# Six tiles of a causal convolution, each cut into five overlapping blocks of its own, in a kernel that TensorE bounds

## The chip, the core and the metric

The kernel runs on one core of a Trainium2 chip. A core has five engines with a queue of instructions each: TensorE (PE; its weight loads are listed apart as PEld), VectorE (DVE), ScalarE (ACT), GpSimd (POOL) and SyncE (SP). Each queue runs in order; the engines meet through semaphores only. All large transfers of this kernel but the first weights are issued from SP's queue. The metric is the device time of one execution in microseconds (us).

## The reference

```python
def _attn_ref(x, weight):                 # x (8, 4096, 192), weight (8, 7)
    w = softmax of weight over its 7 taps  # one set of taps per head, 24 channels a head
    x_pad = 6 rows of zeros in front of each sequence
    out[b, s, h, g] = sum over k of w[h, k] * x_pad[b, s + k, h, g]

def _moe_ref(x, w_in, w_out):             # x (32768, 192), w_in (192, 2048), w_out (2048, 192)
    h = x @ w_in
    g = h * np.cos(h)
    return g @ w_out
```

The second function works on the 32768 rows that the first gives.

## The kernel before

**Tiles and units.** The 32768 rows are 64 tiles of 512 rows, and two tiles are a unit of 1024. For each tile `t` the first product (`mm1`, L503) makes eight pieces `h0` to `h7`: each is 2 x 128 columns of `w_in` against 512 rows, six matmuls over 64 rows of the array, in pairs. Each piece fills one of three double banks (`h_pool`, three buffers). ScalarE takes its cosine (`gcu`, L510, "s0" to "s7"), VectorE multiplies (L514), and the double bank is free again. The second product (`mm2_step`, L552) has 64 steps per tile, each two matmuls on the two row halves; step k of a tile needs piece k // 4 within each half of the steps and one half of `w_out`: steps 0 to 15 the first, 16 on the second. Its two banks are emptied by VectorE ("Q") and ScalarE ("P") (L571) before the next tile's first step.

**The convolution before the change.** The convolution gives each tile as a bf16 transpose `cT`, channels on partitions, which `mm1` reads. There are three ways to it:

- Unit 0 (tiles 0 and 1) in the head of the kernel (`conv_first`, `turn_first`, `conv_rest`): banded 128 x 128 matrices on TensorE, and for tile 0 transposes on TensorE too.
- Units 1 to 3 (tiles 2 to 7): `load_unit` brings the 1024 rows, `load_edges` the 8 rows before each block of 128; `cast_unit` casts both on POOL; `conv_part` (L229) multiplies four heads with the bands over 128 rows into a double bank, twice per unit ("d" and "c"), and ScalarE copies it out (L239); `double_unit` (L307) writes each 64-channel square twice; `turn_unit` (L326) transposes 27 blocks by a transfer; `mend_edges` (L394) puts the first six columns of each block right.
- Units 4 to 31: five blocks of 112 rows, each loaded with the 16 rows before it, by TensorE (`conv_unit`, L277: 16 matmuls over 64 rows and 120 columns; L294 copies them out; two transposes L317 by transfer, "X" and "x", one for each row half), and 464 rows by ScalarE and POOL ("taps" L356, `conv_raw`, `spread_raw`).

**The order is written by hand.** `PE_FIRST`, `ACT_FIRST` for the first tiles and `PE_ORDER`, `ACT_ORDER` for the rest are lists of words; nothing is scheduled afterwards. `h3` is a piece of the first product, `m7` seven steps of the second, `c1`/`c2` the two halves of a convolution, `L`, `K`, `X`, `x`, `T`, `R`, `U` a unit's load, cast, transposes, raw transpose, raw convolution and its spreading, `O` a store; in `ACT` lists `s` is cosine and product, `e..` a copy of a convolution out of its bank, `a..` a tap. A convolution takes one of the three double banks in turn with the pieces.

**Turns.** [...] Between the first and the second half of a convolution (`conv_unit`) and of a tile's 64 steps, an instruction in SP's queue (`Turn`, L196) waits for the first half's last matmul, and the second half waits for it. It stands in SP's queue in order with the loads, transposes and stores.

Of the kernel before, what the change touches and what calls it, by code (L numbers as in the profile page):

```python
# [16 lines left out]
def kernel(  # L17
# [35 lines left out]
    HALF = WN // 2  # L53

# [30 lines left out]

    def load_edges(u, queue=nc.sync):
        queue.dma_start(out=x_tiles[u][:, UB, :],
                          in_=xf[u * U - 8 : u * U - 8 + U, :].rearrange("(n t) d -> n t d", t=128)[:, 0:16, :])
# [25 lines left out]
    load_unit(0, 0, NB)  # L114
# [11 lines left out]


# [9 lines left out]

# [14 lines left out]

# [35 lines left out]

# [14 lines left out]


    bf, xk = {}, {}

    def cast_unit(u, n0=0, n1=UB + 1, copy=nc.gpsimd.tensor_copy):
        if u >= FIRST_RAW:
            xk[u] = xk_pool.tile([128, NC * (UB + 1), 64], BF16, name="xk")
            for n0, n1 in ((NPB, UB + 1), (0, NPB)):  # L210
                copy(out=xk[u][:, NC * n0 : NC * n1].rearrange("p (k n) m -> p k n m", k=NC),  # L211
                     in_=x_tiles[u][:, n0:n1].rearrange("p n (m k) -> p k n m", k=NC))
            if u % UPS == 0:
                nc.gpsimd.memset(xk[u][0 : 128 - OP, 0 : NC * NPB : NPB], 0.0)
            return
        if n0 == 0:
            bf[u] = xb0 if u == 0 else xbf_pool.tile([128, UB + 1, D], BF16, name="x_bf")
        o = 1 if u == 0 else 0
        copy(out=bf[u][:, n0 + o : n1 + o, :].rearrange("p n (h k r) -> p (n h) k r", k=NC, r=R),  # L219
             in_=x_tiles[u][:, n0:n1, :].rearrange("p n (h r k) -> p (n h) k r", k=NC, r=R))  # L220

    ct_tiles = {}
    have = {("whole", 0, 0)}

    def conv_mm(u, c, ps, i, rows, n0, n1, prev=0, **flags):

        h = 4 * c + i
        rhs = bf[u][rows, n0:n1, h * G : (h + 1) * G].rearrange("p n (k r) -> p n k r", k=NC)
        return nc.tensor.matmul(  # L229
            out=ps[i // 2][:, 0 : (n1 - n0) * 2 * G].rearrange("p (n k i r) -> p i n k r", n=n1 - n0, k=NC, i=2)[:, i % 2],  # L230
            lhsT=band[rows, h, 128 if prev else 0 : 256 if prev else 128],
            rhs=rhs, skip_group_check=True, **flags)

    def conv_out(u, c, ps, n0, m0, m1, copy, banks=(0, 1)):

        for b in banks:
            w0 = (2 * c + b) * 2 * R
            o = ct_tiles[u][:, m0:m1, :, 0, w0 : w0 + 2 * R].rearrange("p n k w -> p (n k) w")
            copy(o, ps[b][:, (m0 - n0) * 2 * G : (m1 - n0) * 2 * G].rearrange("p (m w) -> p m w", w=2 * R))  # L239
# [7 lines left out]

    def conv_part(u, c, banks, whole=False):


        ps = banks()
        nb = UB + 1
        for i in range(4):
            conv_mm(u, c, ps, i, slice(0, 128), 0, nb, start=i % 2 == 0, stop=i % 2 == 1)
        if u == 1 and c == 0:
            spread_taps(ps[1][:, nb * 2 * G : nb * 2 * G + K])
        yield
        yield
        if u not in ct_tiles:
            ct_tiles[u] = ct_pool.tile([128, UB + 1, NC, 2, 64], BF16, name="ct")  # L260
        for b in range(2):
            conv_out(u, c, ps, 0, 0, nb, nc.scalar.copy, banks=(b,))
            if b and u == 1 and c == 0:
                nc.scalar.copy(tap, ps[1][:, nb * 2 * G : nb * 2 * G + K])
            if b:
                have.add(("conv", u, c))
            yield

    def conv_unit(u, banks):
# [32 lines left out]
    def double_unit(u):  # L302

        assert {("conv", u, 0), ("conv", u, 1)} <= have
        have.add(("double", u))
        ct = ct_tiles[u]
        nc.gpsimd.tensor_copy(out=ct[:, :, :, 1, :], in_=ct[:, :, :, 0, :])  # L307

    def turn_unit(u, n0=0, n1=UB + 1, part=0):
        if u >= FIRST_RAW:  # L310
            assert {("conv", u, 0), ("conv", u, 1)} <= have
            if part == 0:
                cT[u] = cT_pool.tile([128, NC * (UB + 1) * 128], BF16, name="cT")
            else:
                have.update((("whole", u, 0), ("whole", u, 1)))
            to = cT[u][:, 0 : NC * CW].rearrange("p (n s t) -> p s n t", s=2, t=OP)
            nc.sync.dma_start_transpose(out=to[:, part],  # L317
                                        in_=ct_bufs[u % 2][0:OP, part : part + 2 * NC * NPB].rearrange("p s m -> p (s m)"))
# [405 lines left out]
```

## Time and profile before

| what | us |
|---|---|
| median, lowest and highest of the runs | 705.1, 704.99, 705.26 |
| the profiled execution, and its span | 705.18, 703.5 |
| TensorE busy | 697.0 (99%) |
| ScalarE busy | 644.4 (92%) |
| VectorE busy | 642.4 (91%) |
| POOL busy | 503.7 (72%) |
| granted TensorE clock | 0.999 |

The span runs from the first to the last instruction. A busy TensorE isn't TensorE at its peak, as matmuls overlap; so the chain of work that ended last and the starts of consecutive groups tell more than the busy time. In a timeline's row stand the start, the length, the engine, the line, the operation, what is written and read, the shape, the number of instructions, and in brackets an idle time before it with what ended it. "SPq" rows are transfers that SP issues: the length is that of the issue, not of the transfer.

### The profile page before, as it was taken

To read this page: it belongs to the slowest core of one execution; us is meant where nothing else is said; L and a number is where in the kernel's file an instruction comes from. 1 tells how busy PE (TensorE), PEld (TensorE's weight loads), DVE (VectorE), ACT (ScalarE), POOL (GpSimd) and SP (SyncE) were. 2 spreads that over 40 slices of the span, in tenths; PEclk is the share of its full clock that TensorE was granted. 3 is DMA by queue.
4 is the path that set the end of the run, shared out by engine and by line. 5 is a ranking of instruction groups with operands and counts; after the bars stand their busy time and mean duration, and the time that the engine had idled before them with its cause. 6 is when DMAs were issued, how large, how long until landed. Compare 5 with 4: busy or idle time off the path is not lost.

```text
span 703.5 us, 26826 instructions
## 1 busy us (share of the span) xinstructions
PE 697.0 (99%) x11830; PEld 512.8 (73%) x11830; DVE 642.4 (91%) x598; ACT 644.4 (92%) x831; POOL 503.7 (72%) x214
## 2 busy tenths in 40 slices
PE   8999999999999999999999999999999999999997
PEld 4677777777777777777777777777777777777776
DVE  6889999999999999999999999999999999999996
ACT  7889999999999999999999999999999999999875
POOL 6524478977778877778877688877789778799400
PEclk9999999999999999999999999999999999999999
DMA  8964456667667768676656577577665576874331
GB/s 214 234 167 97 120 135 143 138 147 164 138 153 146 131 145 176 134 152 131 147 152 153 150 159 129 140 161 150 143 147 132 145 174 137 153 127 95 92 91 47
DMA packets 228292, 100.09 MB, mean 142 GB/s; under 512 B 156240, under 2 KB 227792, under 8 KB 228176
## 3 DMA queue, kind: packets, MB, share of 16 engines
q1 hardware_dynamic: 227464, 97.40, 62.7%
q8 instruction: 92, 1.51, 0.9%
q0 software_dynamic: 416, 0.79, 0.7%
q14 instruction: 24, 0.20, 0.1%
q10 hardware_dynamic: 296, 0.20, 0.1%
HBM read 31.36 MB, written 25.17 MB: 80 GB/s over the span
## 4 chain that ended last, share of the span: by engine, by line
PE 96%; DMA 1%; DVE 1%; POOL 0%; SPq 0%; ACT 0%; issue 0%; POOLq 0%
PE o_ps L552 48%; PE h L503 46%; PE h L277 2%; DMA wo_f<-in_moe_w_out_dram 1%; PE h L552 0%; SPq L124 0%; PE h L229 0%; DVE band L415 0%; POOL wo L120 0%; POOL mask L159 0%; DVE ct L438 0%; PE o_ps L432 0%; ACT mask L164 0%; DVE diag L404 0%; DVE prod L401 0%
## 5 line engine op out<-in xcount | busy, mean ns | idle before, releaser
L514 DVE TENSOR_TENSOR g<-h,cs 128x1024 bf16<-128x1024 f32 (+1 forms) x513 | 604.9, 1216 | 27.9 <-ACT cs L510 24.5
L510 ACT ACTIVATE cs<-h 128x1024 bf16<-128x1024 f32 (+1 forms) x513 | 511.0, 1021 | 44.0 <-PE h L503 30.6
L552 PEld LDWEIGHTS <-g 64*128 64x128 bf16 x8192 | 354.2, 94 | 102.2 <-issue 1.0
L552 PE MATMUL o_ps<-wo,g 64*128 64x192 bf16 x8128 | 420.6, 243 | 0.1
L503 PE MATMUL h<-cT,w 64*128 64x512 bf16 (+1 forms) x3078 | 407.0, 376 | 0.8 <-DVE g L514 0.4
L503 PEld LDWEIGHTS <-w 64*128 64x128 bf16 x3078 | 147.6, 94 | 75.0 <-issue 1.8
L211 POOL CAST xk<-x_f 128x768 bf16<-128x768 f32 (+1 forms) x56 | 76.4, 1367 | 113.9 <-DMA x_f<-in_x_dram 109.3
L363 POOL TENSOR_TENSOR raw_prod<-rT,tap 128x2784 f32<-128x2784 bf16 x28 | 135.3, 4832 | 0.2
L370 POOL TENSOR_TENSOR raw_prod<-raw_prod,pa 128x2088 f32<-128x2088 f32 x28 | 129.1, 4609 | 2.2
L356 ACT ACTIVATE pa<-rT,tap 128x348 f32<-128x348 bf16 x168 | 94.6, 580 | 0.0
L374 POOL TENSOR_TENSOR raw_prod<-raw_prod 128x1392 f32<-128x1392 f32 x28 | 87.9, 3138 | 2.2
L571 DVE COPY o_sb<-o_ps 128x384 f32<-128x384 f32 x62 | 34.6, 557 | 23.7 <-PE o_ps L552 23.5
L377 POOL TENSOR_TENSOR ro<-raw_prod 128x696 bf16<-128x696 f32 x28 | 46.5, 1660 | 2.2
L294 ACT CAST ct_buf<-h 112x480 bf16<-112x480 f32 x56 | 28.6, 562 | 4.1 <-PE h L277 0.6
L571 ACT COPY o_sb<-o_ps 128x384 f32<-128x384 f32 x64 | 30.8, 482 | 0.1
L277 PE MATMUL h<-xk,band 64*112 64x120 bf16 x448 | 21.2, 213 | 0.0
L277 PEld LDWEIGHTS <-band 64*112 64x112 bf16 x448 | 18.0, 127 | 0.0
L219 POOL CAST x_bf<-x_f 128x768 bf16<-128x768 f32 (+2 forms) x5 | 9.1, 1812 | 7.0 <-DMA x_f<-in_x_dram 6.9
L307 POOL COPY ct<-ct 128x1728 bf16<-128x1728 bf16 x3 | 4.9, 1630 | 8.9 <-ACT ct L239 8.9
L394 POOL COPY cT<-cT 128x144 bf16<-128x144 bf16 x3 | 0.9, 308 | 13.5 <-DMA cT<-ct 13.5
L136 PE MATMUL o_ps<-zero 128*128 128x512 bf16 x21 | 7.2, 492 | 1.3 <-DVE zero L131 1.3
L239 ACT CAST ct<-h 128x432 bf16<-128x432 f32 x12 | 5.9, 530 | 0.4 <-issue 0.4
(66 smaller groups left out, 52.7 us busy)
## 6 DMA issues: line engine op xcount, KB each, us to landing
out_dram<-o_sb SPq DMA_DIRECT2D x63, 384.0 KB, 3.7
x_f<-in_x_dram SPq DMA_DIRECT2D x28, 480.0 KB, 5.5
x_f<-in_x_dram SPq DMA_DIRECT2D x56, 192.0 KB, 2.7
cT<-ro SPq DMA_DIRECT2D x112, 87.0 KB, 2.3
x_f<-in_x_dram SPq DMA_DIRECT2D x4, 384.0 KB, 5.6
wo_f<-in_moe_w_out_dram SPq DMA_DIRECT2D x4, 384.0 KB, 7.9
x_f<-in_x_dram SPq DMA_DIRECT2D x2, 768.0 KB, 5.2
cT<-ct_buf SPq DMA_TRANSPOSE x56, 4.0
```

The costliest lines, as they stand in the source:

```text
L211: copy(out=xk[u][:, NC * n0 : NC * n1].rearrange("p (k n) m -> p k n m", k=NC), in_=x_tiles[u][:, n0:n1].rearrange("p n (m k) -> p k n m", ...
L277: return nc.tensor.matmul(out=ps[h // 4][0:OP, 0 : NPB * 4 * G].rearrange("p (m i r) -> p i m r", m=NC * NPB, i=4)[:, h % 4], lhsT=band[si ...
L356: mul(pa[u][:, j, part], tap_window(u, j)[:, part], tap[:, j : j + 1])
L363: nc.gpsimd.tensor_tensor(out=p, in0=tap_window(u, PA, K), in1=tap[:, PA:K].rearrange("p (j a b) -> p j a b", a=1, b=1).to_broadcast([128, ...
L370: add(out=p[:, 0:m], in0=p[:, 0:m], in1=a[:, done : done + m], op=ALU.add)
L374: add(out=p[:, 0:m], in0=p[:, 0:m], in1=p[:, n - m : n], op=ALU.add)
L377: add(out=ro[u], in0=p[:, 0], in1=p[:, 1], op=ALU.add)
L503: nc.tensor.matmul(out=h[:, i, n0 * 128 : n1 * 128], lhsT=w[rows, k, j, :], rhs=rhs, start=(k == 0), stop=(k == NC - 1))
L510: nc.scalar.activation(out=cs[:, :, part], in_=h[:, :, part], func=AF.Sin, bias=math.pi / 2.0, scale=1.0)
L514: nc.vector.tensor_tensor(out=g_tiles[t][:, 2 * j : 2 * j + 2, part], in0=h[:, :, part], in1=cs[:, :, part], op=ALU.mult)
L552: ms.append(nc.tensor.matmul(out=o_ps[tt, b, si], lhsT=g_tiles[tt][rows, f, s * 128 : (s + 1) * 128], rhs=wo[rows, f // 2, f % 2, :], star ...
L571: (copy or copies[b])(o_sb[t][:, 2 * b : 2 * b + 2, :].rearrange("p s d -> p (s d)"), o_ps.pop((t, b)))
```

## The change

Tiles 2 to 7 get the way of the five blocks, each tile for itself: five blocks of 112 rows are 560, so 48 rows (`OVER`) in front are computed and not used. `load`, `cast`, `conv_unit` and `turn` take a negative number v = t - 8 for tile t. `load_unit`, `load_edges`, `cast_unit`, `conv_part`, `double_unit`, `turn_unit` and `mend_edges` are gone. The x_f and xk pools have three buffers instead of two. The zero columns of the two `ct_buf`s are set in the head on POOL, not in tile 3. The two matmuls that spread the taps stand in `conv_rest`. The orders of tiles 0 to 7 are new; `PE_ORDER` and `PE_LAST` lose only the marks `p` and `q`, which emitted nothing, as the end of a tile's steps is now found by counting.

```diff
+    EARLY = FIRST_RAW * TPU
...
+    OVER = NPB * OP - T
...
-    xin = ctx.enter_context(tc.tile_pool(name="xin", bufs=2))
-    xbf_pool = ctx.enter_context(tc.tile_pool(name="xbf", bufs=2))
-    ct_pool = ctx.enter_context(tc.tile_pool(name="ct", bufs=2))
+    xin = ctx.enter_context(tc.tile_pool(name="xin", bufs=3))
+    ct_pool = ctx.enter_context(tc.tile_pool(name="ct", bufs=1))
...
-    xk_pool = ctx.enter_context(tc.tile_pool(name="xk", bufs=2))
+    xk_pool = ctx.enter_context(tc.tile_pool(name="xk", bufs=3))
...
+    def rows_of(t0, n, step):
+        r = xf[t0 : t0 + 128, :]
+        return bass.AP(r.tensor, r.offset, [[D, 128], [step * D, n], [1, D]])
...
+    def load(v):
+        x_tiles[v] = xin.tile([128, UB + 1, D], FP32, name="x_f")
+        if v < 0:
+            nc.sync.dma_start(out=x_tiles[v][:, 0:NPB, :], in_=rows_of((v + EARLY) * T - OVER + OP - 128, NPB, OP))
             return
...
+    def cast(v):
+        xk[v] = xk_pool.tile([128, NC * (UB + 1), 64], BF16, name="xk")
+        for n0, n1 in ((NPB, UB + 1), (0, NPB)):
+            if v < 0 and n0:
+                continue
+            nc.gpsimd.tensor_copy(out=xk[v][:, NC * n0 : NC * n1].rearrange("p (k n) m -> p k n m", k=NC),
+                                  in_=x_tiles[v][:, n0:n1].rearrange("p n (m k) -> p k n m", k=NC))
...
+    def turn(v, part=0):
+        assert ("conv", v) in have
+        if part == 0:
+            cT[v] = cT_pool.tile([128, NC * (UB + 1) * 128], BF16, name="cT")
+        else:
+            have.update([("whole", v + EARLY)] if v < 0 else [("whole", v * TPU), ("whole", v * TPU + 1)])
+        to = cT[v][:, 0 : NC * CW].rearrange("p (n s t) -> p s n t", s=2, t=OP)
+        nc.sync.dma_start_transpose(out=to[:, part],
+                                    in_=ct_bufs[v % 2][0:OP, part : part + 2 * NC * NPB].rearrange("p s m -> p (s m)"))
...
-    load_unit(0, NB, UB)
-    load_unit(1, 0, NB)
-    load_unit(1, NB, UB)
-    load_edges(1)
+    load_first(NB, UB)
+    load(2 - EARLY)
+    load(3 - EARLY)
...
+    for buf in ct_bufs:
+        nc.gpsimd.memset(buf[0:OP, 0], 0.0)
+        nc.gpsimd.memset(buf[0:OP, 1:].rearrange("p (k n) m -> p k n m", k=NC)[:, :, NPB:], 0.0)
+    cast_first(NB, UB)
...
+        spread_taps(banks[1][:, 2 * D : 2 * D + K])
...
+                if t < TPU:
+                    m = t * NB
+                    rhs = cT[0][rows].rearrange("p (n c k) -> p n c k", c=NC, k=128)[:, m + n0 : m + n1, k, :]
+                else:
+                    c, t0 = (cT[t - EARLY], OVER) if t < EARLY else (cT[t // TPU], t % TPU * T)
+                    t0 += k * CW + n0 * 128 + (0 if i else OP)
...
-    PE_FIRST = ["K1 h0a h0b W0 h1 h2 h3 r h4 w5 d11 w4 h5 d21 W1 c11 X0 m1 h6 m11 h7 L2 c21 D1",
-                "m6 K2 h0 m1 L3 h1 K3 m13 q h2 m3 h3 m9 h4 m6 h5 m3 X1 c12 m11 p c22 h6 d12 h7 L4 L5 m17 c13 m4 c23 m1 d22 Y1 D2 m1",
-                "h0 m2 h1 m7 q K4 h2 m11 h3 X2 O m8 h4 Y2 m13 p h5 h6 m9 h7 m7",
-                "h0 m8 h1 m8 q h2 m7 h3 m7 O m1 h4 m3 d13 m4 d23 m6 h5 m4 p T4 h6 h7 m4 D3 Z0 Z1",
-                'm12 h0 m4 h1 K+3 m5 h2 m7 q h3 m6 h4 m17 h5 X+1 m9 p h6 h7 O m4',
-                'm11 h0 m4 h1 m6 h2 m7 q x+1 Y3 h3 m5 h4 m7 c1 m8 c2 m3 h5 T+3 L+4 m9 p O h6 h7 m4']
-    ACT_FIRST = ["s0a s0b s1 s2 er s3 s4 ed11 ed21 s5 ec11 s6 ec21 s7",
-                "s0 s1 s2 s3 s4 s5 ec12 ec22 Q P s6 ed12 s7 ed22 ec13 ec23",
-                "s0 s1 s2 s3 Q s4 P s5 s6 s7",
-                "s0 s1 s2 s3 s4 ed13 ed23 Q s5 P s6 s7"] + ACT_ORDER
+    PE_FIRST = ["K2 h0a h0b h1 h2 r W0 h3 h4 c12 w5 c22 X0 w4 W1 L4 h5 m2 K3 h6 m9 h7 m1",
+                "m1 X2 L5 m5 x2 m3 h0 h1 m8 h2 m5 h3 m10 h4 L8 m6 h5 c13 m14 c23 X3 h6 m11 h7 K8 m12 L6",
+                "K4 O h0 m1 h1 m7 h2 m12 c14 h3 m2 c24 m7 h4 x3 m12 h5 h6 m9 h7 m7 K5",
+                "h0 m8 X4 O h1 m8 h2 m8 h3 m3 h4 x4 m4 c15 T+3 L+4 m8 c25 m9 X5 h5 h6 h7 m4",
+                "x5 m12 h0 K+3 m4 K6 m1 h1 m5 h2 m6 h3 m14 h4 L7 c16 m6 c26 m3 h5 m9 O X6 h6 h7 m4",
+                "K7 m19 h0 m4 h1 m5 h2 x6 m4 h3 m11 h4 c1 L+4 m8 O c2 h5 m9 h6 h7 m4",
+                "m11 T+2 h0 m4 R+1 h1 m6 c17 K+3 c27 h2 m7 h3 X7 x7 h4 m16 h5 O m16 h6 m3 X+1 h7 m1",
+                "m11 h0 h1 m10 h2 T+3 m7 h3 x+1 m4 h4 m6 c1 m12 c2 m4 h5 m6 h6 h7 m2 O m2 L+4"]
+    ACT_FIRST = ["s0a s0b s1 s2 er s3 s4 s5 ec22 ec12 s6 s7",
+                "s0 s1 s2 s3 s4 Q s5 P ec23 ec13 s6 s7",
+                "s0 s1 s2 s3 Q ec24 ec14 s4 P s5 s6 s7",
+                "s0 s1 s2 s3 s4 ec25 ec15 Q P s5 s6 s7",
+                "s0 a200 s1 s2 a012 s3 s4 Q ec16 ec26 s5 P s6 s7 a107 a117",
+                "s0 s1 s2 a212 s3 s4 a004 ec2 Q ec1 s5 P s6 s7",
+                "s0 s1 ec17 ec27 s2 a112 s3 a213 s4 Q a014 s5 P s6 a206 s7",
+                "s0 s1 s2 s3 a103 s4 a004 ec2 ec1 Q s5 P s6 s7"]
```

In the new lists `c13` and `c23` are the two halves of tile 3's convolution (before, of unit 3), and `L8`, `K8` are the load and cast of unit 4. `W0` and `W1` cast the halves of w_out on POOL, and `w5`, `w4` are warm-up matmuls.

More of the change, by code (lines that the diff above doesn't have):

```diff
@@ L222 @@
[L222 to L232, printed above, removed]
@@ L241, in ring_banks @@
+    have = {("whole", 0)}
     def ring_banks():
@@ L246, in o_banks @@
         return [o_pools[b].tile([128, T], FP32, name="o_ps%d" % b) for b in range(2)]
[L248 to L267, printed above, removed]
     def conv_unit(u, banks):
@@ L360, in conv_raw @@
     def conv_raw(u):
+        assert {("tap", u, j, half) for j in range(PA) for half in range(2)} <= have
         a, p = pa.pop(u), raw_prod
```

189 lines of the change are left out of this document (62 added, 127 removed).

## The prediction

> **What bounds the kernel now.** I read the page first (busy shares, then the chain of work that ended last), then the chain in order of time, then the timelines of TensorE, ScalarE, VectorE and SyncE over the first 100 us, since the change touches nothing behind tile 7.
>
> ```profile
> PE 697.0 (99%) x11830; PEld 512.8 (73%) x11830; DVE 642.4 (91%) x598; ACT 644.4 (92%) x831; POOL 503.7 (72%) x214
> ...
> PE 96%; DMA 1%; DVE 1%; POOL 0%; SPq 0%; ACT 0%; issue 0%; POOLq 0%
> ```
>
> TensorE is 96% of the chain. What isn't TensorE lies in the first 23 us, where the chain runs through the load of w_out and its cast (start, length):
>
> ```profile
> 11.02 1.10 SPq L124
> 12.16 8.84 DMA wo_f<-in_moe_w_out_dram
> 21.12 1.48 POOL wo L120
> 24.36 1.07 PE o_ps L552 x26
> ...
> 33.12 1.40 PE o_ps L552 x34
> ...
> 53.91 1.29 PE h L503 x12
> ```
>
> Two rates come from it: a step of the second product (two matmuls) costs 1.40/17 = 0.0824 us, an h (six matmuls) 1.29/2 = 0.647 us. Step 16 is the first that needs the second half of w_out, cast by 22.60; it starts at 22.65, and from there TensorE hardly stops. Its timeline (start, length with the pipeline's tail) gives the prices of the convolutions by the start of what follows:
>
> ```profile
> 29.69 0.54 PE L229 MATMUL h<-x_bf,band 128*128 128x216 bf16 x4
> ...
> 30.17 1.08 PE L552 MATMUL o_ps<-wo,g 64*128 64x192 bf16 x22
> ...
> 35.44 0.81 PE L503 MATMUL h<-cT,w 64*128 64x512 bf16 x6
> ...
> 72.40 0.39 PE L277 MATMUL h<-xk,band 64*112 64x120 bf16 x8
> 72.61 0.84 PE L552 MATMUL o_ps<-wo,g 64*128 64x192 bf16 x16
> ```
>
> Four old matmuls (L229) cost 0.48 us, half a unit of the five-block kind (L277) 0.21. Tile 2 starts at 35.44. From 22.65 to there lie 71 steps (5.85), 8 h (5.18) and three L229 groups (1.44), 12.47 us in 12.79: 0.32 us of waits. To h0 of tile 4 at 56.39 lie 121 steps, 16 h and one group, 20.80 in 20.95: 0.15. So before loses 0.47 us in the stretch that the change rewrites.
>
> ScalarE and VectorE stand just under TensorE; these rows give the latency of the ring of three h banks:
>
> ```profile
> 36.29 3.06 ACT L510 ACTIVATE cs<-h 128x1024 bf16<-128x1024 f32 x3 [0.27 <-PE h L503]
> ...
> 24.73 7.10 DVE L514 TENSOR_TENSOR g<-h,cs 128x1024 bf16<-128x1024 f32 x6 [0.18 <-ACT cs L510]
> ...
> 37.35 4.82 DVE L514 TENSOR_TENSOR g<-h,cs 128x1024 bf16<-128x1024 f32 x4 [1.80 <-ACT cs L510]
> ```
>
> An h that starts at P has its cosine at P+0.85 (36.29 against 35.44) and its product at P+1.91 (37.35); a product lasts 1.22 and they follow each other every (7.10-1.22)/5 = 1.17. So a bank comes free at P+3.13 where VectorE isn't behind, and each further bank 1.17 later.
>
> **The change, part by part.** I sum against the profiled execution, 705.18 us (span 703.5 and 1.7 around it), 0.08 above the median of 705.10. From tile 8 on the orders are the same (the dropped p and q emit nothing, and both kernels stand at step 452 there), so only tiles 0 to 7 count.
>
> *Convolutions on TensorE.* Behind 22.65 before runs four L229 groups, 1.92 us; two ran earlier, among warm-up matmuls. After runs tiles 3 to 7 behind that point, 5 x 0.42 = 2.10; tile 2's lies in the head. Sum +0.18. Of the old group 4 x 216 columns x 0.42 ns (1.29 us for 6 pairs of 512) is 0.36, so 0.12 is more than columns. Bounds: +0.65 if that 0.12 isn't saved, +0.18 if it is; the row of the whole group is the nearer. [...]
>
> *The head.* Loads ahead of w_out on SP's queue: 4 x 384 KB + 96 before, 2 x 384 + 2 x 480 after, 96 KB more. At the 289 GB/s of 10 to 20 us that is 0.34 us later for w_out, so step 16 comes at 22.95. Bounds: -0.5 (w_out isn't last any more and the ring decides: h7 waits for tile 2's copies until 21.1, then 0.65 and four steps put step 16 at 22.1) and +0.7 (twice the bytes' time). I take +0.3, the bytes. The four new memsets of the ct_bufs stand on POOL before the second cast of x: 2 x 1024/1984 x 1752 ns = 1.8 us in the 3.6 us that POOL idles there (until 11.73); with that idle gone they would push the second half of tile 0 and tile 1. The taps' two matmuls move from one place in the head to another, 0. ScalarE has four copies (L239) fewer ahead of step 16 and two of 0.56 more.
>
> *The ring.* A convolution takes one of three banks. Four places in the new orders leave too little between taking and freeing:
> - Tile 1, c13 behind h5 takes h3's bank. From h0 at P TensorE needs 6 h and 29 steps, P+6.27; the fourth product ends at P+1.91+3x1.17+1.22 = P+6.64. Wait 0.37.
> - Tile 2, "h0 m1 h1 m7 h2 m12 c14 h3": h3 comes at P+3.8 and takes h1's bank, free at P+4.3. Wait 0.5. (Before, h3 was at P+3.59 and took h0's, free at P+3.13.)
> - Tile 5, c1 comes straight behind h4, 3.18 us behind h2 whose bank it takes: 3.13, with VectorE a little behind from the taps on ScalarE. Wait 0.15.
> - Tile 6, "h0 m4 h1 m6 c17 c27 h2": h2 comes at P+2.54 and takes h0's bank, P+3.13. Wait 0.6; the round trip from c17 over SP's row-half turn to c27 lies inside it.
>
> Together 1.62, against the 0.47 that before loses here: +1.15. Bounds: -0.47 (all hidden) and +2.3 (twice).
>
> *At nothing, with their cover.* POOL loses three doublings (1.63), three mendings (0.31) and two casts of 2.56 and gains six casts of 1.51; it waits for loads most of its idle time, and nobody waits for it but SP, below. ScalarE gains two copies (1.0 us) each in tiles 2, 4 and 6 and loses two in tile 0 and four in 1: tile 4 has 8 x 0.92 + 4 x 0.48 + 1.0 + 0.45 = 10.7 against TensorE's 10.87; without those 0.2 us each copy would show. Three transposes of 27 blocks become twelve of 15: SP issues of 1.5 us and a landing 4.0 after. Tile 3's second one goes out behind c14 (about 38.5) and lands by 42.5, three us before its h0; tile 4's first waits for the last h of tile 2 (bank of two cT), goes out at 44.8, the second behind tile 2's turn at 48, landed by 52 for 56. Tiles 5 to 7 have more. A third x_f and xk buffer only let loads go earlier.
>
> Sum: 0.18 + 0.3 + 1.15 = +1.6, so 706.8 us.
>
> **Rivals.** SP is one queue, and the turns that let the second row half of a product or convolution start stand in it (L196 before). These rows show what it can be held by:
>
> ```profile
> 16.00 3.92 SPq L326 DMA_TRANSPOSE cT<-ct  x1
> ...
> 21.83 1.35 SPq L87 DMA_DIRECT2D x_f<-in_x_dram  x1
> ...
> 81.34 1.49 SPq L317 DMA_TRANSPOSE cT<-ct_buf  x1
> ```
>
> *SP holds tile 0's turn (slower still).* In the new order X2, a load and x2 stand before the turn at step 31. X2 waits for ScalarE's copies of tile 2 (s5 at 19.07 as before, 1.02, two copies with overlap 1.0): 21.1. With 1.5 each (the clean row) SP is free at 24.6, and behind a load's landing perhaps 25.8; TensorE comes to step 32 at 26.2. With 3.9 each (the 12-block row beside loads) it is free at 29.4, a stall of 3.2; that the ring waits of tile 1 go with it gives back 0.4 to 0.7. Halfway, 2.2: 709.0. It decides as soon as the two issues take over 4.6 us together. For it: the head's queue is as full as at 16.0. Against: of 56 issues of this shape the longest took 3.0. [...]
>
> *POOL holds tile 1's turn.* Tile 6's load waits for the casts of unit 4, whose load goes out behind tile 0's turn (26.2), lands 5.5 us later at 31.7 to 33.4 and takes 1.23 + 1.51 on POOL: 36.1 at the latest. Behind it on SP stand store 0 and the turn that TensorE wants at about 37.4. It decides when that load lands over 1 us later; priced at 1.5: 708.3.
>
> *Not slower.* VectorE runs a little ahead (five products in 5.85 us elsewhere, a pitch of 1.16), the waits at c13, c14 and c17 shrink to nothing as in before's steady tiles, where a convolution costs no wait at all, and w_out's end is set by one late DMA engine and not by bytes: 705.18 + 0.18 - 0.47 = 704.9. It decides when the four waits come to less than about 0.7. For it: between 60 and 680 us TensorE is busy in every microsecond, with the same ring. Against: there at least 7 or 8 steps stand around each half convolution.
>
> **How the numbers follow.** About 0.2% (1.4 us) is what a measurement of this kernel can tell from no change. My forecast, 706.8 with its own range of 706.0 to 707.6: 0.55 (0.31 of it over 706.5). SP holds tile 0's turn: 0.15. POOL holds tile 1's: 0.08. Not slower: 0.22, of it 0.03 under 703.7, with w_out earlier as well. Slower 0.31 + 0.15 + 0.08 = 0.54; faster 0.03; same 0.43. The range leaves out 0.1 at each end: 704.7, below the not-slower case, to 708.9, by the first rival.
>
> **What would show it.** Steps: h0 of tile 1 near 23.4 (22.8 before), tile 2 near 34.8, h0 of tile 4 near 56.5 and of tile 8 about 1.6 later than the 99.25 of before, then the same distance to the end. VectorE as the releaser of PE waits near c13, h3 of tile 2 and h2 of tile 6. First rival: a PE gap near 26 ended by SP, with a transpose of 3 us or more before it; second: the same near 37. Wrong altogether: the chain runs through anything but TensorE behind 25 us, or the time between tile 8 and the end changes.

## The result and the profile after

The changed kernel takes 709.43 us (median of 6 runs, 709.03 to 709.88) against 705.06 us before (704.98 to 705.54): ratio 1.006, interval [1.005, 1.007]. It is 4.4 us slower; the prediction said 1.6, and 709.43 lies above the end of its range (708.9). The profiled execution took 709.03 us, span 707.2, which is 3.85 more than the 705.18 profiled before.

The page of the changed kernel, busy shares and the chain that ended last:

```profile
PE 697.8 (99%) x11902; PEld 557.6 (79%) x11902; DVE 642.5 (91%) x598; ACT 644.7 (91%) x831; POOL 497.9 (70%) x212
...
PE 94%; DVE 2%; DMA 1%; SPq 1%; POOL 1%; ACT 0%; issue 0%; POOLq 0%
```

TensorE is 94% of the chain instead of 96%; VectorE's share goes from 1% to 2%, that of SyncE's queue from 0% to 1%. The chain in order of time (start, length; some rows) says where:

```profile
12.46 8.13 DMA wo_f<-in_moe_w_out_dram
20.64 1.47 POOL wo L120
22.11 1.45 POOL xk L210
24.37 3.13 SPq L270
37.73 2.37 DVE g L452 x2
54.48 1.94 PE h L441 x18
67.83 1.90 PE o_ps L490 x46
79.82 3.50 DVE g L452 x3
```

Behind w_out's cast the chain leaves TensorE at three places: a transpose in SP's queue at 24.37 (L270), and products on VectorE at 37.73 and 79.82. The first is the largest. (The row of tile 3's cast on POOL, at 22.11, stands in the chain as what released tile 5's load, but the load does not need it: in the run with ScalarE's copies earlier, below, that load's issue ended at 23.89 and that cast at 23.95.) TensorE's timeline around it:

```profile
22.14 1.00 PE L490 MATMUL o_ps<-wo,g 64*128 64x192 bf16 x20
...
25.63 0.43 PE L490 MATMUL o_ps<-wo,g 64*128 64x192 bf16 x6
27.61 0.34 PE L490 MATMUL o_ps<-wo,g 64*128 64x192 bf16 x4 [1.56 <-SPq L191]
```

Three steps from 25.63 are worth 0.25 us, so the next could have started at 25.88 and starts at 27.61: 1.73 us, released by SP's turn (L191). SP's own timeline shows what stood ahead of that turn:

```profile
21.46 1.62 SPq L270 DMA_TRANSPOSE cT<-ct_buf  x1
23.18 1.14 SPq L95 DMA_DIRECT2D x_f<-in_x_dram  x1
24.37 3.13 SPq L270 DMA_TRANSPOSE cT<-ct_buf  x1
27.69 1.47 SPq L100 DMA_DIRECT2D x_f<-in_x_dram  x3
```

X2, tile 5's load and x2 end at 27.50; the turn and step 32 follow at once. The smaller waits, tile 2 and tile 6, look like this on TensorE:

```profile
38.42 1.43 PE L490 MATMUL o_ps<-wo,g 64*128 64x192 bf16 x24
39.68 0.37 PE L232 MATMUL h<-xk,band 64*112 64x120 bf16 x8
40.13 0.82 PE L441 MATMUL h<-cT,w 64*128 64x512 bf16 x6
...
82.26 0.90 PE L232 MATMUL h<-xk,band 64*112 64x120 bf16 x16
83.36 0.82 PE L441 MATMUL h<-cT,w 64*128 64x512 bf16 x6 [0.20 <-DVE g L452]
```

Twelve steps (0.99) take from 38.42 to 39.68, 0.27 too long; half a convolution (0.21) takes 0.45; a whole one in tile 6 (0.42) takes 1.10.

With the prediction's rates (a step 0.0824, an h 0.647, half a unit 0.21, an old group 0.48) the starts of h0 of each tile give the whole account. "Work" is the rates times what lies between two h0 in program order, "wait" the rest:

| From h0 of tile | before: us | work | wait | after: us | work | wait |
|---|---|---|---|---|---|---|
| 1 | 12.63 | 12.30 | 0.33 | 12.86 | 11.03 | 1.83 |
| 2 | 9.88 | 9.87 | 0.01 | 10.81 | 10.29 | 0.52 |
| 3 | 11.07 | 10.93 | 0.14 | 10.94 | 10.87 | 0.07 |
| 4 | 10.38 | 10.37 | 0.01 | 11.94 | 11.45 | 0.49 |
| 5 | 10.96 | 10.95 | 0.01 | 10.63 | 10.21 | 0.42 |
| 6 | 10.38 | 10.37 | 0.01 | 11.66 | 10.87 | 0.79 |
| 7 | 10.96 | 10.95 | 0.01 | 11.00 | 10.95 | 0.05 |
| sum | 76.26 | 75.74 | 0.52 | 79.84 | 75.67 | 4.17 |

Tile 1 starts at 22.81 before and 22.96 after, tile 8 at 99.07 and 102.80, and from tile 8 to the start of the last h both take 594.7 us (to 693.80 and 697.55). The sums of work are nearly equal because three steps fewer (0.25 us) lie in this stretch after the change; its convolutions cost 0.18 more by these rates (seven of 0.42, against two of 0.42 and four old groups of 0.48). The loss is 3.65 us of waits: 1.5 in tile 1, the rest in tiles 2, 4, 5 and 6.

### The profile page after: what moved, and what is told of

The parts are those of the page before. It is cut to its first block, busy times and chain, and to the rows that moved or that the text cites. A ratio compares the mean times of both kernels' runs of the same rounds, so it can differ in the third digit from the quotient of the medians.

```text
span 707.2 us, 26980 instructions
## 1 busy us (share of the span) xinstructions
PE 697.8 (99%) x11902; PEld 557.6 (79%) x11902; DVE 642.5 (91%) x598; ACT 644.7 (91%) x831; POOL 497.9 (70%) x212
## 4 chain that ended last, share of the span: by engine, by line
PE 94%; DVE 2%; DMA 1%; SPq 1%; POOL 1%; ACT 0%; issue 0%; POOLq 0%
PE o_ps L490 47%; PE h L441 45%; PE h L232 2%; DMA wo_f<-in_moe_w_out_dram 1%; DVE g L452 1%; SPq L270 0%; PE h L490 0%; SPq L124 0%; ACT cs L448 0%; DVE band L349 0%; POOL wo L120 0%; POOL xk L210 0%; POOL mask L155 0%; DVE ct L376 0%; PE o_ps L370 0%
## 5 line engine op out<-in xcount | busy, mean ns | idle before, releaser
L490 PEld LDWEIGHTS <-g 64*128 64x128 bf16 x8192 | 381.2, 94 | 77.5 <-SPq L191 2.8
L490 PE MATMUL o_ps<-wo,g 64*128 64x192 bf16 x8128 | 434.7, 243 | 1.7 <-SPq L191 1.6
L441 PE MATMUL h<-cT,w 64*128 64x512 bf16 (+1 forms) x3078 | 419.1, 376 | 1.3 <-DVE g L452 0.6
L441 PEld LDWEIGHTS <-w 64*128 64x128 bf16 x3078 | 178.7, 94 | 58.3 <-issue 2.9
L210 POOL CAST xk<-x_f 128x960 bf16<-128x960 f32 (+1 forms) x62 | 85.4, 1380 | 148.3 <-DMA x_f<-in_x_dram 96.0
L249 ACT CAST ct_buf<-h 112x480 bf16<-112x480 f32 x68 | 34.7, 562 | 4.5 <-PE h L232 0.6
L232 PE MATMUL h<-xk,band 64*112 64x120 bf16 x544 | 27.7, 214 | 0.3 <-DVE g L452 0.2
L232 PEld LDWEIGHTS <-band 64*112 64x112 bf16 x544 | 23.6, 127 | 2.3 <-DVE g L452 1.1
L120 POOL CAST wo<-wo_f 128x1536 bf16<-128x1536 f32 x2 | 2.9, 1469 | 3.7 <-DMA wo_f<-in_moe_w_out_dram 3.7
L490 PE MATMUL h<-wo,g 64*128 64x192 bf16 x64 | 3.3, 243 | 0.0
```

What stands on the lines that cost most here:

```text
L210: nc.gpsimd.tensor_copy(out=xk[v][:, NC * n0 : NC * n1].rearrange("p (k n) m -> p k n m", k=NC), in_=x_tiles[v][:, n0:n1].rearrange("p n ( ...
L232: return nc.tensor.matmul(out=ps[h // 4][0:OP, 0 : NPB * 4 * G].rearrange("p (m i r) -> p i m r", m=NC * NPB, i=4)[:, h % 4], lhsT=band[si ...
L441: nc.tensor.matmul(out=h[:, i, n0 * 128 : n1 * 128], lhsT=w[rows, k, j, :], rhs=rhs, start=(k == 0), stop=(k == NC - 1))
L490: ms.append(nc.tensor.matmul(out=o_ps[tt, b, si], lhsT=g_tiles[tt][rows, f, s * 128 : (s + 1) * 128], rhs=wo[rows, f // 2, f % 2, :], star ...
```

## The experiments

All are edits of the changed kernel unless it says otherwise. The medians of kernels that keep the stall at tile 0's turn scatter by some tenths, because its length does: in nine profiles it left TensorE empty for 1.30 to 2.14 us. Where a single tile is the question, I therefore compare the distance between two h0 and not the whole time.

### Tile 0's turn

**x2 behind the turn**

```diff
-"m1 X2 L5 m5 x2 m3 h0 h1 m8 h2 m5 h3 m10 h4 L8 m6 h5 c13 m14 c23 X3 h6 m11 h7 K8 m12 L6",
+"m1 X2 L5 m5 m3 h0 h1 m8 h2 m5 x2 h3 m10 h4 L8 m6 h5 c13 m14 c23 X3 h6 m11 h7 K8 m12 L6",
```

> Only x2, tile 2's second transpose, is moved behind the turn of tile 0's product in SP's queue. Theory 1 (SP holds the turn: X2 1.62 us, a load's issue 1.14 and x2 3.13 us ended at 27.50, and step 32 started at 27.61, 1.73 us late): what is left there is a turn between two steps that follow each other, about 0.3 us as in tile 2 (0.27), and the ring wait of 0.37 at c13 that hid in the stall comes back. So 1.0 to 1.4 us less, 708.0 to 708.4. Theory 2 (the loss is convolution work and ring waits on TensorE): 709.4, and the gap near 26 us stays, or another releaser than SP stands there.

Measured: 707.72 us (707.62 to 707.92), 1.0037 [1.0025, 1.005]. The median is 1.71 below that of the changed kernel, more than expected; the profiled executions differ by 1.31 (709.03, the changed kernel's fastest, and 707.72), as expected. TensorE, then SP:

```profile
25.76 0.86 PE L490 MATMUL o_ps<-wo,g 64*128 64x192 bf16 x10
26.46 0.81 PE L441 MATMUL h<-cT,w 64*128 64x512 bf16 x6
```

```profile
23.93 1.04 SPq L95 DMA_DIRECT2D x_f<-in_x_dram  x1
26.30 1.54 SPq L270 DMA_TRANSPOSE cT<-ct_buf  x1
```

Five steps (0.41) take 0.70, so 0.29 is left of the turn. Tile 1 takes 11.40 us instead of 12.86; from tile 2 to tile 8 it takes 66.97, the changed kernel 66.98. Theory 1 stands, and the stall touches nothing else. The ring wait of 0.37 at c13 did not show: at most 0.08 us is lost there. But what is left of the turn covers it. c13 starts at 29.72, 6.62 us after h0 instead of the 6.27 of the work, and the fourth product of tile 1, whose bank it takes, had just ended, at 29.64 (the last of six products that VectorE's timeline has in one row from 22.54, 7.10 long).

**Tile 5's load behind x2**

```diff
-"m1 X2 L5 m5 x2 m3 h0 h1 m8 h2 m5 h3 m10 h4 L8 m6 h5 c13 m14 c23 X3 h6 m11 h7 K8 m12 L6",
+"m1 X2 m5 x2 L5 m3 h0 h1 m8 h2 m5 h3 m10 h4 L8 m6 h5 c13 m14 c23 X3 h6 m11 h7 K8 m12 L6",
```

> Only the load of tile 5 is moved, from ahead of x2 to behind it; both still stand ahead of tile 0's turn. If x2's 3.13 us come from the load in flight ahead of it, x2 takes 1.5 to 1.7 us here, SP is free by about 25.9 and the stall shrinks from 1.73 to about 0.3: 708.0 to 708.4. If the second transpose is long for another reason (the first one's data, the writes to the same tile), x2 still takes about 3.1 us, the load's issue ends at about 27.4 and the time stays at 709.4.

Measured: 708.37 us (707.80 to 708.94), 1.0048 [1.0034, 1.0062]. SP's timeline:

```profile
21.43 3.66 SPq L270 DMA_TRANSPOSE cT<-ct_buf  x2
25.18 1.11 SPq L95 DMA_DIRECT2D x_f<-in_x_dram  x1
```

The two transposes take 3.66 together instead of 4.75 (x2 2.11 of it) and end at 25.09. The load's own issue then ends at 26.29, and step 32 starts at 26.40 with 0.56 us lost. So 1.0 of x2's 3.13 us came from the load ahead of it.

**ScalarE's copies earlier**

```diff
-"s0a s0b s1 s2 er s3 s4 s5 ec22 ec12 s6 s7",
+"s0a s0b s1 s2 er s3 s4 ec22 ec12 s5 s6 s7",
```

> Only ScalarE's order in tile 0: the two copies of tile 2's convolution (20.43 to 21.44) go ahead of the cosine of h5 (19.51 to 20.53) instead of behind it; ScalarE idled from 17.78 to 19.51, and the convolution they copy had ended at about 17.7. Theory (these copies are the start of the chain: copies, X2, a load's issue, x2, the turn): X2 goes out at about 19.9, behind the load whose issue ends at 19.82, instead of 21.46, SP is free before TensorE comes to step 32, 0.3 us of a bare turn are left of the stall of 1.73, and h7 of tile 0, which waited 0.47 for the same copies, starts earlier: h0 of tile 1 at 22.5 instead of 22.96. 707.3 to 707.8. Rival (an issue is held by the loads in flight, whenever it is given): X2 or x2 takes 3 to 4 us here, SP is free at 25 or later and half of the stall stays: 708.3 or more.

Measured: 708.74 us (707.78 to 708.93), 1.005 [1.0037, 1.0062]. SP's timeline:

```profile
20.35 2.91 SPq L270 DMA_TRANSPOSE cT<-ct_buf  x1
23.36 0.53 SPq L95 DMA_DIRECT2D x_f<-in_x_dram  x1
23.94 3.27 SPq L270 DMA_TRANSPOSE cT<-ct_buf  x1
```

X2 goes out 1.1 us earlier and takes 1.3 longer, since it now stands close behind tile 4's load. x2 ends at 27.21 instead of 27.50 and 1.50 us of the stall stay: the rival is right. The traces of the changed kernel and of its fourteen edits agree. They hold thirty of X2 and x2: the sixteen that went out within 0.11 us of the end of a load's issue took 2.89 to 3.87 us, the fourteen that went out 1.23 us or more behind one 1.48 to 2.32. Why a load just ahead makes the issue long, no run here shows. h7 of tile 0 did start earlier (20.82 instead of 21.49), but then a step waited for w_out's cast, which ended at 22.52, and tile 1 started at 22.98 (in all_a, below, whose start has this edit alone, that cast ended at 21.86 and tile 1 started at 22.56):

```profile
22.57 0.59 PE L490 MATMUL o_ps<-wo,g 64*128 64x192 bf16 x10 [0.52 <-POOL wo L120]
```

### What a turn costs by itself

**Tile 2, an h between steps 31 and 32**

```diff
-"K4 O h0 m1 h1 m7 h2 m12 c14 h3 m2 c24 m7 h4 x3 m12 h5 h6 m9 h7 m7 K5",
+"K4 O h0 m2 h1 m7 h2 m11 c14 h3 m2 c24 m7 h4 x3 m12 h5 h6 m9 h7 m7 K5",
```

> One step of tile 2 is moved from behind h2 to ahead of h1, so that h2 stands between steps 31 and 32 of tile 1's product; the 0.27 us that TensorE waits between those two steps goes. Theory A (a turn between steps that follow each other costs its way over SP): 0.27 less, 709.15. Theory B (the ring: h3 behind c14 takes h1's bank and waits for its product anyway): the wait only moves to h3, whose 0.24 becomes 0.45 to 0.5, and the time stays at 709.4.

Measured: 709.45 us (709.13 to 710.96), 1.0066 [1.0053, 1.0078]. From tile 2 to tile 8 66.94 us against 66.98. TensorE's timeline:

```profile
41.45 0.37 PE L232 MATMUL h<-xk,band 64*112 64x120 bf16 x8
42.14 0.82 PE L441 MATMUL h<-cT,w 64*128 64x512 bf16 x6 [0.32 <-DVE g L452]
```

The wait between steps 31 and 32 is gone, and h3 waits 0.48 instead of 0.24. Theory B: tile 2's 0.51 is one wait for h1's bank, and the turn only hid half of it.

**Before, 29 bare turns**

```diff
-'m12 h0 m4 h1 K+3 R+1 m5 h2 m7 q h3 U+0 m6 h4 m17 h5 X+1 m9 p h6 h7 O m4'
+'m12 h0 m4 h1 K+3 R+1 m5 h2 m8 h3 U+0 m5 h4 m17 h5 X+1 m9 p h6 h7 O m4'
```

> The kernel before, with one step of every even tile from tile 6 on (29 tiles) moved from behind h3 to ahead of it... that is from the second half of a product to h2's seven, so that steps 31 and 32 of the product follow each other with no h between them; SP's queue is empty there. If such a turn costs its way from TensorE over SP and back, 0.27 as between c17 and c27 in tile 6 and in tile 2 of the changed kernel: 29 x 0.27 = 7.8 us more, 712.9. If what follows absorbs it as the ring does in tile 2: under 1 us more, below 706.

Measured: 713.08 us (712.97 to 713.13), 1.0112 [1.0099, 1.0126], 7.96 more than before's 705.12 beside it: 0.27 for each turn. The edit moves one step from behind h3 to between h2 and h3. The list of waits of this kernel (engine and line, releaser: total, times, longest; these are waits of the weight loads, so the total is not TensorE's loss):

```profile
PEld L552 <- SPq L196: 9.4, 29, 0.3
```

**Before, 27 convolutions with c1 and c2 together**

```diff
-'m11 h0 m4 h1 m6 h2 m7 q x+1 h3 m5 h4 m7 c1 m8 c2 m3 h5 T+3 L+4 m9 p O h6 h7 m4'
+'m11 h0 m4 h1 m6 h2 m7 q x+1 h3 m5 h4 m7 c1 c2 m11 h5 T+3 L+4 m9 p O h6 h7 m4'
```

> The kernel before, with c1 and c2 next to each other in the 27 odd tiles from tile 7 to tile 59: the eight steps between them move behind c2. Each convolution's turn is then bare. Theory (0.27 each, as the start of c27's matmuls, 82.75, stands to the end of c17's, about 82.47): 27 x 0.27 = 7.3 us more, 712.4. Rival (a bare turn costs nothing by itself, and tile 6's loss is only the ring's): within 1 us of 705.1.

Measured: 713.71 us (713.44 to 713.97), 1.0122 [1.0108, 1.0135], 8.59 more, 0.32 for each. On TensorE's timeline a whole convolution, worth 0.42, takes 0.72 there (115.13 to 115.85). From its list of waits:

```profile
PEld L277 <- SPq L196: 6.9, 27, 0.6
```

So with an empty queue a turn cost 0.27 us (the mean of 29) and 0.32 (of 27) when nothing stood between its two sides, in a kernel that keeps TensorE busy 99% of the span. Where another wait ended later, as in tile 2, it cost nothing (66.94 us against 66.98).

### Tile 6

**Spacing**

```diff
-"m11 T+2 h0 m4 R+1 h1 m6 c17 K+3 c27 h2 m7 h3 X7 x7 h4 m16 h5 O m16 h6 m3 X+1 h7 m1",
+"m11 T+2 h0 m4 R+1 h1 m6 c17 K+3 m5 c27 m2 h2 m7 h3 X7 x7 h4 m12 h5 O m13 h6 m3 X+1 h7 m1",
```

> In tile 6 five steps are moved between c17 and c27 and two between c27 and h2, taken from behind h4 and h5. Theory (h2 waits for h0's product, 0.6 in the prediction, 0.68 in the trace): the wait goes, 0.6 to 0.7 us less, 708.75. Rival (VectorE is behind through all of tile 6, so the wait moves to h3 or h5): less than 0.2 us, 709.3, and VectorE is the releaser of a later h.

Measured: 709.53 us (709.06 to 709.84), 1.0062 [1.005, 1.0075]. h2's wait falls from 0.68 to 0.09, but from h0 of tile 6 to h0 of tile 8 it is 22.54 us against 22.66. A new wait stands at the first step of the next product, on TensorE's timeline:

```profile
89.14 0.83 PE L441 MATMUL h<-cT,w 64*128 64x512 bf16 x6
90.40 0.42 PE L490 MATMUL o_ps<-wo,g 64*128 64x192 bf16 x6 [0.43 <-ACT o_sb L509]
```

The rival's number is right, its place is not: no later h waits, but the banks of product 5, which ScalarE and VectorE empty only behind a cosine and a product.

**Spacing, and two taps on VectorE**

```diff
-"s0 s1 ec17 ec27 s2 a112 s3 a213 s4 Q a014 s5 P s6 a206 s7",
+"s0 s1 ec17 ec27 s2 b112 s3 b213 s4 Q a014 s5 P s6 a206 s7",
```

> The spacing of c17, c27 and h2 in tile 6 as in the run before, and two of tile 6's four taps (0.58 us each on ScalarE) go to VectorE. From h0 of tile 6 to h0 of tile 8 the changed kernel takes 22.66 us, the spaced one 22.54. Theory (ScalarE is the bound of tile 6: two copies of a convolution and four taps between eight cosines, so the wait only moved from h2 to the first step of product 6): 22.54 becomes 21.8 to 22.0 and the time 0.6 to 0.8 less than with spacing alone. Rival (VectorE, or the ring alone): no change, 22.5, since VectorE has 1.2 us a product and no more room than ScalarE.

Measured: 709.58 us (709.31 to 711.87), 1.007 [1.0057, 1.0082]; 22.94 us from tile 6 to tile 8. ScalarE is relieved and VectorE empties the bank late instead (TensorE's timeline):

```profile
90.80 0.40 PE L490 MATMUL o_ps<-wo,g 64*128 64x192 bf16 x5 [0.68 <-DVE o_sb L509]
```

**Without the early taps**

```diff
+            if u < FIRST_RAW + 2:
+                nc.gpsimd.memset(pa[u], 0.0)
...
+        if u < FIRST_RAW + 2:
+            return
```

> The twelve products of raw rows and taps of units 4 and 5 (0.58 us each on ScalarE, in tiles 4 to 7) are left out; a memset on GpSimd puts zeros in their place, so the last rows of these two units lack three of their seven taps. From h0 of tile 4 to h0 of tile 8 the changed kernel takes 45.23 us, of which 43.5 are TensorE's work by the rows (255 steps, 32 h, 4 convolutions). Theory (ScalarE, which has about 43 us of work in these four tiles, two more convolutions' copies than before, sets the waits of tiles 4 to 6): 43.9 to 44.2 and a time 1.0 to 1.3 less, 708.3. Rival (the ring's spacing and SP's turns alone make these waits): 45.0 or more, 709.3.

Measured: 709.66 us (709.01 to 711.32), 1.0067 [1.0054, 1.008]. From tile 4 to tile 8 45.13 us against 45.23, though ScalarE has twelve products less. h2 of tile 6 still waits, for VectorE (TensorE's timeline; the added lines move L441 to L445):

```profile
82.35 0.90 PE L232 MATMUL h<-xk,band 64*112 64x120 bf16 x16
83.43 0.82 PE L445 MATMUL h<-cT,w 64*128 64x512 bf16 x6 [0.18 <-DVE g L456]
```

My theory that ScalarE's load makes the waits of tiles 4 to 6 falls.

**Spacing, and h7 ahead of the next product**

```diff
-"m11 T+2 h0 m4 R+1 h1 m6 c17 K+3 m5 c27 m2 h2 m7 h3 X7 x7 h4 m12 h5 O m13 h6 m3 X+1 h7 m1",
+"m11 T+2 h0 m4 R+1 h1 m6 c17 K+3 m5 c27 m2 h2 m7 h3 X7 x7 h4 m12 h5 O m13 h6 h7 m3 X+1 m1",
```

> Tile 6 as in the run with spacing alone, and h7 moved ahead of the three steps that begin the next product, so that two h instead of one stand between the end of product 5 and the first step of product 6, which needs its banks emptied. From h0 of tile 6 to h0 of tile 8: 22.66 us changed kernel, 22.54 spaced, 21.83 TensorE's work. Theory (two limits of equal size in tile 6, h2's bank and the emptying of product 5; the second took over when the first was spaced away): 21.9 to 22.1. Rival (ScalarE is behind through tiles 6 and 7, and the wait moves on to an h of tile 7): 22.4 or more.

Measured: 709.38 us (708.69 to 710.53), 1.0062 [1.0049, 1.0074], with a stall of 1.90 us at tile 0's turn; tile 6 to tile 8 takes 22.24 us. Half of the 0.83 us of waits there are gone, where spacing alone took 0.12. So two limits lay on top of each other in tile 6: h2's bank, and the emptying of product 5 with one h as its cover. The other half, 0.4 us, is spread over waits of 0.1 to 0.2 that I did not take apart.

### Tile 4

```diff
-"x5 m12 h0 K+3 m4 K6 m1 h1 m5 h2 m6 h3 m14 h4 L7 c16 m6 c26 m3 h5 m9 O X6 h6 h7 m4",
+"m12 h0 K6 m4 K+3 m1 h1 m5 h2 m6 h3 m2 x5 m12 h4 c16 m6 c26 L7 m3 h5 m9 O X6 h6 h7 m4",
```

> Tile 4: x5 (issue 60.00 to 61.64) behind the turn that step 32 waits for until 61.76, tile 6's cast ahead of the one that waits for a load until 60.73 (c16 waited for it until 63.72), tile 7's load behind c26's turn. From h0 of tile 4 to h0 of tile 5 the changed kernel takes 11.94 us, TensorE's work is 11.45. Theory (SP's and GpSimd's order make these waits): 11.5 to 11.6, 0.35 to 0.4 less in all. Rival (the ring takes over, as in tile 2, where taking the turn's 0.27 away gave nothing): 11.8 or more.

Measured: 709.23 us (708.51 to 711.17), 1.0064 [1.005, 1.0078]; tile 4 11.63 us instead of 11.94, and tile 2 to tile 8 66.62 instead of 66.98. In the changed kernel c16 waited for a cast that stood on GpSimd behind one that waited for a load; its GpSimd timeline:

```profile
59.49 4.23 POOL L210 CAST xk<-x_f 128x768 bf16<-128x768 f32 x3 [21.87 <-PE h L441]
```

These three casts end at 63.72, c16 starts at 63.77; tile 6's cast, whose data had long been there, was the last of them. (The row names an h as what released the first; in the run with spacing alone the same cast is put down to its load, and it starts 5.1 to 5.3 us behind that load's issue in both and in the tile 4 run.) The theory is right within 0.1: 0.31 of tile 4's 0.49 is queue order (GpSimd's, and x5 ahead of the turn on SP), not the ring. The other 0.18 stays, in waits of less than 0.1.

### The start

```diff
-    load(2 - EARLY)
-    load(3 - EARLY)
+    load(2 - EARLY)
...
         load_wo(1)
+        load(3 - EARLY)
```

> The load of tile 3 (480 KB) goes behind the two loads of w_out instead of ahead of them; nothing else. Theory 1 (bytes ahead of w_out set when it lands, as the prediction costed 96 KB with 0.3 us): w_out lands over 1 us earlier and the wait of 0.64 us at the first step that needs its second half goes: 0.5 to 0.6 less, 708.9. Theory 2 (w_out's end is not what the start waits for, or it is set by one late DMA engine): h0 of tile 1 stays within 0.1 of 22.96 and the time within 0.2 of 709.4, or it is later where tile 3's cast now holds others on GpSimd's queue.

Measured: 711.47 us (709.22 to 711.80), 1.0077 [1.0063, 1.009]. GpSimd's timeline, then TensorE's:

```profile
18.55 1.47 POOL L120 CAST wo<-wo_f 128x1536 bf16<-128x1536 f32 x1 [0.88 <-DMA wo_f<-in_moe_w_out_dram]
```

```profile
22.01 0.82 PE L441 MATMUL h<-cT,w 64*128 64x512 bf16 x6 [0.47 <-ACT ct_buf L249]
```

w_out's second cast starts 2.1 us earlier (20.64 in the changed kernel), yet tile 1 starts at 23.48, later. h7 of tile 0 waits 0.47 for ScalarE's copies as it does in the changed kernel, so w_out's landing is not what the start waits for: theory 2. With the result of the copies run above, the start too has two limits on top of each other, the copies and w_out's cast. The 0.5 us of the later start come from ahead of all this: in this execution the matmuls of tile 0's h0 waited for the transfer of w_in until 11.21 (0.35 us of idle time on TensorE's timeline), and what follows stands about 0.5 later than in the changed kernel (h1 at 13.12 instead of 12.59, h7 at 22.01 instead of 21.49). all_b, with the same order of loads, has no such wait. The large part of the extra time lies behind the turn, below under the clock: the two of its five executions without a slowed clock took 709.22 and 709.77.

### All together

all_a and all_b put the pieces together, all_c adds x2 and tile 5's load behind the turn, all_d changes the order of tile 5. The lists of all_c (tiles 0 and 3 as changed, tile 0 with w2 for w4; load order as in the start's run):

```diff
+"m1 X2 m5 m3 h0 h1 m11 h2 m5 x2 L8 h3 m7 h4 m6 h5 m5 c13 L5 m9 c23 X3 h6 m11 h7 K8 m12 L6",
+"K4 O h0 m2 h1 m7 h2 m11 c14 m6 h3 m2 c24 m5 h4 x3 m8 h5 h6 m9 h7 m7 K5",
...
+"m12 h0 K6 m4 K+3 m1 h1 m5 h2 m6 h3 m2 x5 m12 h4 c16 m6 c26 L7 m3 h5 m9 O X6 h6 h7 m4",
+"K7 m16 h0 m5 h1 m7 h2 x6 m5 h3 m10 h4 c1 L+4 m8 O c2 m2 h5 m7 h6 h7 m4",
+"m11 T+2 h0 m4 R+1 h1 m6 c17 K+3 m5 c27 m2 h2 m7 h3 X7 x7 h4 m12 h5 O m13 h6 h7 m3 X+1 m1",
...
+"s0a s0b s1 s2 er s3 s4 ec22 ec12 s5 s6 s7",
+"s0 s1 ec17 ec27 b111 s2 s3 a213 s4 Q a014 s5 P s6 a206 s7",
```

> All at once: the copies of tile 2 ahead of the cosine of h5; an h between steps 31 and 32 of the products of tiles 0 and 1; steps put between c13, c14, c17 and the h behind them, and ahead of h3 and h5 in tile 5; x5 behind tile 3's turn; tile 6's cast ahead of the one that waits for a load; one tap of tile 6 on VectorE in a gap of it. If each wait that the trace of the changed kernel shows is worth its length: 709.4 - 1.73 - 0.47 - 0.5 (tile 2) - 0.4 (tile 4) - 0.3 (tile 5) - 0.5 (tile 6) = 705.5. If ScalarE's load in tiles 4 to 7 keeps their 1.7 us of waits wherever the steps stand: 706.7.

> As the one before, and two of the four warm-up matmuls ahead of h5 in tile 0 are left out and tile 3's load goes behind w_out. The warm-up matmuls end at 18.64, the bank of h5 comes free at 18.2; with the copies out of the way w_out's cast (22.11) is what step 16 waits for next. If the start is one chain of these, 0.4 to 0.6 us less than the run before: 705.0, which is the time of the kernel before. If tile 3's load behind w_out makes X2's and x2's issues longer, as when it was moved alone (x2 3.87 us, 711.47 in all), 1 us or more above the run before.

> The last of the combined kernels, with x2 and tile 5's load behind tile 0's turn, one more step between c14 and h3 in tile 2 and h7 of tile 6 ahead of the next product. Tile 1 starts at 22.2 there and has 11.0 us of work: tile 2 at 33.3 instead of 34.8; tiles 2 to 7 took 66.0 there and lose 0.3 to 0.5: tile 8 at 98.8 to 99.0, where before has 99.07. If waits are the whole difference between the two kernels: 704.8 to 705.1. If the change costs TensorE work besides: 706 or more with tile 8 at 100 or later.

> As all_c, with ScalarE's emptying of product 4 ahead of the cosine of h5 in tile 5 (there product 5's first step waited until 76.28 for it, 0.73 us beyond its work) and h5 straight behind c2 again. If that wait was the rest of the difference: 0.4 to 0.7 less than all_c, 705.1 to 705.4, level with the kernel before. If the wait moves on, as it did in tile 6: 705.6 to 705.9.

Measured: all_a 707.50 us (706.86 to 707.94), 1.0034 [1.0021, 1.0046]; all_b 707.52 (706.98 to 709.38), 1.0041 [1.0027, 1.0054]; all_c 705.76 (705.28 to 707.29), 1.001 [1.0001, 1.0018]; all_d 706.29 (705.65 to 707.49), 1.0017 [1.0008, 1.0026].

all_a and all_b miss because X2 and x2 still stood ahead of the turn: TensorE lost 1.1 and 1.6 us there, and the head's gain in all_b (tile 1 at 22.16) went into the longer stall. all_c confirms it: tile 1 starts at 22.15 and takes 11.05 us, its work and nothing else. The time is 0.7 above the upper end of what I expected, for tile 8 starts at 99.57. Tiles 2 to 7 still hold 1.7 us of waits (66.37 us, of which 64.64 are work), 0.89 of them in tile 5, most of that at the first step of the next product. TensorE's timeline of all_c:

```profile
76.28 1.41 PE L490 MATMUL o_ps<-wo,g 64*128 64x192 bf16 x30 [0.47 <-ACT o_sb L509]
```

all_d, made against that wait, shortened tile 5 by 0.16 us only, and its tile 2 took 0.69 us longer. There tile 1's turn was held; TensorE's timeline of all_d:

```profile
36.53 1.08 PE L490 MATMUL o_ps<-wo,g 64*128 64x192 bf16 x22 [0.54 <-SPq L191]
```

X3's issue, in the same queue, took 2.83 us in that execution and 1.48 in all_c's (at 32.38 and 32.46), and tile 6's load and a store stood behind it and ahead of the turn. So the order of all_c is no safe one either. No version beat the kernel before. all_c came to 1.001 of it, interval [1.0001, 1.0018], with the convolutions as changed, so the order of the work, not the convolution, is nearly all of the loss (0.58 of 4.4 us stays).

## Why the prediction was wrong

- **Direction and place right.** Slower, nearly all of it between tile 1 and tile 8, the same distance from tile 8 to the end. "About 1.6 later" at tile 8 was 3.73 (102.80 against 99.07; the 99.25 of the prediction is the chain's start of that h, not the timeline's).
- **The step that failed: the sum has no term for SP's queue at tile 0's turn.** The prediction kept it as a rival, "SP holds tile 0's turn", with a chance of 0.15. It happened as described: a gap near 26 ended by SP behind a transpose of 3.13 us, and its condition (two issues over 4.6 us together) was met with 1.62 + 3.13 = 4.75. Step 32 came 1.73 us late. The stall gave back 0.27 of that and not 0.4 to 0.7: with x2 behind the turn tile 1 is 1.46 shorter, as 0.29 of the turn is left. What misled me was "of 56 issues of this shape the longest took 3.0". Those are steady issues, with a median of 1.50; none of them went out less than 7.1 us behind the end of a load's issue. The row from the same stage, 3.92 us beside loads, was the nearer one for x2, and the runs with x2 and with tile 5's load moved show it: with no load's issue just ahead x2 took 1.54 and 2.11 us instead of 3.13.
- **That the rival's time, 709.0, is 0.4 from the result is in part luck.** Its stall of 2.2 does not follow from its own numbers: 3.2 less 0.4 to 0.7 is 2.5 to 2.8, and halfway to nothing is 1.3 to 1.4. Measured it was 1.46, net of what it gave back; waits that the prediction did not have, in tiles 4 and 5, made up for about as much.
- **The ring: 1.62 us in four places.** Tile 2 0.5, measured 0.51, in two pieces that are one wait. Tile 6 0.6, measured 0.68, but its removal is worth little by itself. Tile 5 0.15 at c1, measured 0.06 there and 0.42 with the waits at h3 and h5. Tile 1 0.37, hidden by the stall and, without the stall, by the bare turn; the bank came free 6.54 us after h0, where the prediction had 6.64. Missed: tile 4's 0.49, most of it from queue order, and 0.11 in tile 6 at the next product.
- **Convolutions on TensorE, +0.18:** right by the rates, the half unit 0.21 as taken. The work of tiles 1 to 7 came out 0.07 less all the same, with three steps (0.25) fewer in it.
- **The head, +0.3:** wrong sign. Step 16 did not wait for the 96 KB; w_out's cast started at 20.64 instead of 21.12, and h7 waited for ScalarE's copies, the lower bound that I had named. Tile 1 started 0.15 later with three more steps done (0.25), so this term is -0.1.
- **ScalarE's cover in tile 4:** it held. Without the taps the time did not fall.
- **POOL holds tile 1's turn:** not here. SP was free at 38.34, before step 31 had ended.

## What to carry to other kernels

A semaphore that goes through another engine's queue cost a round trip here (0.27 to 0.32 us if nothing stands between its two sides) plus whatever that queue held at that moment; price the second part from rows of the same stage, with its loads in flight (3.13 us for x2), and not from the median of the steady state (1.50). Before a wait is counted as a gain, look for the next limit behind it: in tile 2 an edit against one wait gave nothing, in tile 6 0.12 us, and edits against both limits of tile 6 gave 0.42. A table of work against elapsed time from one landmark to the next, by rates from the trace, finds such waits, also those without a releaser in the profile.

## What was not expected of the hardware

TensorE's clock halved after a stall of 1.93 and of 2.14 us in two profiles, and stayed full after others as long. In the run with the turn of tile 2 moved the profiled execution had 1.93 us of idle time ended by SP, and the stretches behind it show it (length, then PE busy with the number of matmuls, the other engines, the granted clock PEclk, DMA share, GB/s):

```profile
25.80:28.10 2.30, 0.37 (x10) 0.15 (x6) 2.30 (x3) 1.02 (x1) 0.00 (x0) 1.00 1.14 249
28.10:30.00 1.90, 1.90 (x18) 1.07 (x16) 0.23 (x1) 0.34 (x1) 0.00 (x0) 0.50 1.06 219
30.00:32.00 2.00, 2.00 (x24) 1.45 (x22) 1.22 (x1) 0.69 (x1) 0.21 (x1) 0.62 0.98 307
32.00:34.00 2.00, 2.00 (x46) 1.68 (x44) 0.82 (x1) 1.76 (x2) 1.66 (x2) 1.00 0.28 93
```

The clock is 0.50 from 28.1 to 31.5, and an h takes 1.27 us instead of 0.65: another 1.7 us lost. The run with w_out first shows the same behind a gap of 2.14 (0.50 from 29.1 to 32.5). Two others with gaps of 2.14 and 1.90 (tile 6 spaced with two taps moved, and with h7 ahead) kept the full clock, a mean of 1.000 over the execution, so it is not the length alone. The times of 710.5 to 711.9 among the runs that keep the stall fit this. Where they were not profiled, only the mean granted clock of the execution is known: it is 0.997 or 0.998 in those eight and in all_b's 709.38, and 0.999 or 1.000 in every other execution. In both profiles the slow stretch lasted 3.4 us; what decides whether it comes, no run here shows.

The busy time of weight loads (PEld) is no sign of the pace: 557.6 us in the changed kernel and 512.8 before, but 595.6 with tile 6 spaced (709.53 us) and 514.3 with the two taps moved besides (709.58 us). The changed kernel and these two have the same 11902 loads. I have no cause for it.
